# A recurrent attention feeding a gated MLP: one attention visit per chunk with two PSUM banks, one bank for the first MLP product, and x turned through memory

## The chip, the core and the metric

The kernel runs on one core of a Trainium2 chip. The core has TensorE (matrix products, results in PSUM, a memory of 8 banks of 512 fp32 values on each of 128 partitions), VectorE, ScalarE, GpSimd (which doesn't reach PSUM), and SyncE, whose queue (SP) issues most DMA transfers. The engines run their own instruction lists in order and wait for one another by semaphores. The metric is the device time of one execution in microseconds; lower is better.

## What is computed

There are 4 batches, 8 heads, 768 steps and a head width of 48. A recurrence over the steps gives y:

```python
state = np.zeros((B, H, D, D))
for t in range(S):
    cur = np.einsum('bhd,bhe->bhde', u[None] * k[:, :, t], v[:, :, t])
    y[:, :, t] = np.einsum('bhd,bhde->bhe', r[:, :, t], state + cur)
    state = w[None, :, :, None] * state + np.einsum('bhd,bhe->bhde', k[:, :, t], v[:, :, t])
```

With x = y laid out as 4 x 768 x 384, an MLP along the time axis of low rank (32) and one along the channels follow:

```python
h = xt @ U @ V                       # xt: x with time and channel exchanged
u = x + h.transpose(0, 2, 1)
out = u + np.maximum(u @ w_ch1, 0.0) @ w_ch2   # 384 -> 1536 -> 384
```

U, V, w_ch1 and w_ch2 arrive as 64-bit floats.

## The kernel before

**Attention.** Each batch is cut into 6 chunks of 128 steps, each of two sub-chunks of 64. Heads go in pairs: an even head lies on the lower 64 partitions, an odd head on the upper 64. For a chunk n, `p_sc` makes the scores of r and k and `p_su` the products of k and v that go into the state; both write the banks `pab` (PSUM tags `tr` and `sc`, one for each of two halves). VectorE reads them: `a_am` masks the scores, `a_st` makes the next state. `p_out` then makes the output rows: masked scores times v (`av`, with `vsw` a copy of v of the odd heads with sub-chunks exchanged), and r times the state (`sq`). All are matmuls of at most 64 x 64, which use only a quarter of the array each; the program alternates two lists of them (`in_turn`) that stand in different row halves of the array.

A chunk is done in two TensorE operations, the two parts of `a_part` (L864). Each alternates one row half of chunk n's output with the other half of chunk n+1's scores and state products. Both parts accumulate into one bank, `pav` (tag `av`, for every other chunk of batch 0 `mm`). Since two row halves may not write one bank at once, a copy of one element of `pav` by ScalarE or VectorE (`seen`, L903) stands between the parts: the second part's first matmul waits for it. `a_x` (L925) adds `pav` and the diagonal term `dv` into x.

**Between attention and MLP.** G = Uᵀx is summed over the batch's chunks: in batch 0 chunk by chunk in the bank of the wake matmuls (`c_gx`, `c_g0`), in the others in one operation (`c_g`, bank `pG`). u must stand with channels on partitions, split into a high part `uTh` in the type fp32r and the rest `uTl`. For the first half of a batch's steps, `c_x` (L1027) turns x with nine TensorE transposes into three banks, and `c_xu` (L1041) accumulates V·G on top and splits. For the second half of batches 1 to 3, `c_u` adds h to x, `c_store` writes it to memory in blocks of 32 x 32, `c_blocks` reads it back, and `c_turn` turns the blocks on VectorE.

**MLP.** All matmuls are fp32r with operands split in two. One unit is `m_1` (L1102): a first product of 9 matmuls of 128 x 128 x 384 into a bank of tag `mm` (two of them), then ScalarE's relu into `hh` and VectorE's `hl` = max(p, 0) - `hh`, which reads the bank again; and `m_2`: 9 matmuls into three `acc` banks. The units are issued as m_1(0), m_1(1), m_2(0), m_1(2), m_2(1) and so on, 24 pairs for each batch. Before each batch's first m_2 three matmuls V·G (`gate`) open the `acc` banks. In batch 0 each weight block is also loaded, turned from 64-bit floats (`raw_w`, on ScalarE and VectorE) and split into `w1s` and `w2s`.

**The order.** A planner in the program (class `Plan`) gets every operation with an engine, a cost estimate, its buffers and a due time, and lays out each engine's list by simulating the engines: an engine takes the ready operation with the earliest due time. An operation that may run on GpSimd or VectorE (`on_either`) goes where it would be done sooner. Due times are set in units of PER = 1.95: batch 0's MLP starts at T0 = 46, its attention chunks are 5.5 apart (EACH), those of batch 1 are 8 apart and those of batches 2 and 3 are 11. So a batch's attention is woven into the MLP of the batch before it. While batch 0 starts up, the planner puts dummy matmuls (`wake`, `wake2`) into gaps of TensorE.

The eight PSUM banks before: `mm` 2, `acc` 3, `tr` 1, `sc` 1, `av` 1.

Of the kernel before, what the change touches and what calls it, by code (L numbers as in the profile page):

```python
# [9 lines left out]
F32 = mybir.dt.float32  # L10
# [278 lines left out]
def rwkv_moe(ctx: ExitStack, tc: tile.TileContext, r, k, v, w, u, U, V, w1, w2, out):  # L289
# [42 lines left out]
    def bank(tag, name):  # L332
        return Buf(ps, [128, 512], F32, tag, {"mm": 2, "acc": 3}.get(tag, 1), name)
# [5 lines left out]
    opened = []  # L339

    def whole(*args, **kw):

        opened.clear()
        return nc.tensor.matmul(*args, **kw)  # L344
# [285 lines left out]
    def a_load(n):  # L630
        b, c = divmod(n, NCH)
        if n < 4:
            t3 = xbuf([128, 2 * H * HP + DM], F32, "uTl" if n % 2 else "uTh", 2, f"ld_{n}")

            def part(i):
                if i < 2:
                    return t3.t[:, i * H * HP:(i + 1) * H * HP].rearrange("p (h d) -> p h d", h=H)
                return t3.t[:, 2 * H * HP:].rearrange("p (h d) -> p h d", h=H)
            ts = [(t3, i) for i in range(3)]
# [13 lines left out]
        for i, src in enumerate((r, k, v)):  # L653
            eng = "ACT" if n < 3 and i == 1 else "SP"
            dma(lambda q, i=i, src=src: q.dma_start(part(i)[:, :, :D], src[b, :, c * C:(c + 1) * C, :].rearrange("h p d -> p h d")),  # L655
                [ts[i] if n < 4 else (t3, i)] if n < 4 else [(ts[i], "d")], [], 1024, 192, eng=eng)
        rs[n], ks_[n], vs[n] = [((lambda i=i: part(i)), ([(t3, i), (t3, f"pad{i}")] if n < 4 else [(ts[i], "d"), (ts[i], f"pad{i}")])) for i in range(3)]
# [69 lines left out]
    def a_tr(n, i):  # L727
# [18 lines left out]
        def turn(q0, q1):  # L746
            opened.clear()
# [34 lines left out]
    avp = {}  # L782
# [26 lines left out]
    ROWS = (1, 0)  # L809

    def p_out(n, row):
# [4 lines left out]
        pt = avp[n]  # L816
# [5 lines left out]
        def av(q, j, i):  # L822
# [3 lines left out]
                                    start=(row == ROWS[0] and q == 0), stop=False, skip_group_check=True)  # L826

        def sq(q, i):
            rows = head_rows(row)
            return nc.tensor.matmul(to(q, row, i), lhsT=rT.t[rows, q, i * C2:(i + 1) * C2], rhs=St[n, i].t[rows, q, :],  # L830
                                    start=False, stop=(row == ROWS[1] and q == NP - 1), skip_group_check=True)
# [15 lines left out]
    def reads(n, j, i):  # L847

        return [*trs[n], kss[n], *vs[n][1]]

    seen = {}

    def a_first(n):

        abs_[n] = [bank(t, f"pab_{n}_{j}") for j, t in enumerate(AB)]
        a, b_ = p_sc(n, 0) + p_su(n, 0), p_sc(n, 1) + p_su(n, 1)
        pe(1000, lambda: in_turn(a, b_), abs_[n], reads(n, 0, 0), tiled=True)
        ams[n] = [None, None]
        for j in range(2):
            a_am(n, j)  # L860
        for i in range(2):
            a_st(n, i)

    def a_part(n, part):  # L864

        nxt = (n + 1) % NCH
        last = n % NCH == NCH - 1
        row = ROWS[part]
        if part == 0:
            if nxt:  # L870
                abs_[n + 1] = [bank(t, f"pab_{n + 1}_{j}") for j, t in enumerate(AB)]
            avp[n] = bank("mm" if front(n) and n % 2 else "av", f"pav_{n}")
        o = 1 - row
        mine = p_out(n, row)
# [520 lines left out]
```

## Time and profile before

| what | value |
|---|---|
| median of 3 runs | 427.16 us (426.8 to 429.48) |
| span of the profiled execution, first to last instruction | 426.3 us |
| TensorE busy | 415.6 us, 98% |
| VectorE, ScalarE, GpSimd busy | 264.5, 137.3, 63.6 us |
| relu `hh`, 96 times on ScalarE | 47.1 us |
| `hl`, 96 times on VectorE | 53.0 us |
| first MLP matmul of batch 0 | 53.65 us |

The page gives the profiled execution by its span; its own time is not listed beside it. In the profile a busy TensorE means that some matmul was under way; since matmuls overlap, the distance between starts tells what one costs, not its length. `Lnnn` is a line of the kernel; MLP matmuls all stand at L344 (a helper), so tiles tell them apart: `p` is an MLP product, `pab` and `pav` belong to attention, `pu`, `ph` and `pG` to the step between. The small fp32 matmuls of attention leave two records each.

### The profile page before, as it was taken

The numbers are of one execution on the slowest core, as the hardware profiler recorded it, in microseconds if no ns is written. First come the engines' busy times: TensorE is split into PE (matmuls) and PEld (weight loads), VectorE is DVE, ScalarE is ACT, GpSimd is POOL, SyncE is SP. The second block draws the span as 40 slices with busy tenths as digits, with TensorE's granted clock in tenths as the row PEclk, the third lists the DMA queues.
The fourth block names the chain that finished last, engine by engine and source line by source line (L and its number), as shares of the span: only waits on it lengthen the run. The fifth ranks groups of instructions, "written<-read, shape, count | busy, mean of one in ns | idle before, by whom it ended". The sixth has DMA issues, their size and how long they took to land.

```text
span 426.3 us, 12170 instructions
## 1 busy us (share of the span) xinstructions
PE 415.6 (98%) x5122; PEld 397.3 (93%) x5122; DVE 264.5 (62%) x598; ACT 137.3 (32%) x374; POOL 63.6 (15%) x100
## 2 busy tenths in 40 slices
PE   8998999999999999999999999999999999999994
PEld 8888899999999999999999999999999999999994
DVE  6888897599999838676785466576622452113122
ACT  2876695276541314112112221322112221111110
POOL 2654220053521003011100001101100000000000
PEclk9998899999999999999999999999999999999999
DMA  9979977697458676755477664231100420001001
GB/s 144 157 148 246 250 177 147 158 260 179 83 85 180 113 162 102 139 90 84 104 147 118 104 153 60 47 66 31 57 2 2 75 92 2 0 0 58 0 2 62
DMA packets 181951, 43.53 MB, mean 102 GB/s; under 512 B 168961, under 2 KB 180354, under 8 KB 181890
## 3 DMA queue, kind: packets, MB, share of 16 engines
q1 hardware_dynamic: 176706, 41.21, 48.2%
q10 hardware_dynamic: 5184, 1.48, 1.9%
q8 instruction: 42, 0.69, 0.7%
q14 instruction: 19, 0.16, 0.1%
HBM read 36.18 MB, written 6.49 MB: 100 GB/s over the span
## 4 chain that ended last, share of the span: by engine, by line
PE 84%; DMA 5%; SPq 5%; DVE 2%; ACT 1%; issue 1%; DVEq 0%; ACTq 0%
PE p L344 72%; SPq L655 4%; PE pav L824 4%; DMA raw_w<-in_moe_w_ch_dram 3%; PE pav L830 3%; PE pab L788 2%; PE pu L344 1%; DMA ub<-in_u_dram 1%; PE pab L803 1%; SPq L515 1%; DMA wT<-in_w_dram 1%; PE pG L995 1%; SPq L667 1%; DMA raw_v<-in_moe_V_dram 1%; DVE raw_w L543 0%
## 5 line engine op out<-in xcount | busy, mean ns | idle before, releaser
L344 PE MATMUL p<-uTh,w1s 128*128 128x384 f32 x576 | 148.2, 338 | 0.0
L1118 DVE SCALAR_TENSOR_TENSOR hl<-p,hh 128x384 fp32r<-128x384 f32 x96 | 53.0, 552 | 113.7 <-ACT hh L1117 113.5
L344 PE MATMUL p<-w2s,hh 128*128 128x384 f32 x576 | 119.3, 340 | 0.0
L1117 ACT ACTIVATE hh<-p 128x384 fp32r<-128x384 f32 x96 | 47.1, 490 | 207.2 <-PE p L344 207.2
L344 PEld LDWEIGHTS p<-uTh,w1s 128*128 128x128 f32 x576 | 103.0, 188 | 0.8
L344 PEld LDWEIGHTS p<-w2s,hh 128*128 128x128 f32 x576 | 99.9, 188 | 1.6
L344 PE MATMUL p<-uTl,w1s 128*128 128x384 f32 x288 | 96.5, 335 | 0.0
L344 PE MATMUL p<-w2s,hl 128*128 128x384 f32 x288 | 65.9, 334 | 0.0
L344 PEld LDWEIGHTS p<-uTl,w1s 128*128 128x128 f32 x288 | 54.0, 188 | 0.3 <-DVE uTl L1050 0.3
L344 PEld LDWEIGHTS p<-w2s,hl 128*128 128x128 f32 x288 | 51.4, 188 | 0.0
L824 PE MATMUL pav<-vsw,am 64*64 64x48 f32 x384 | 32.9, 224 | 0.1
L824 PEld LDWEIGHTS pav<-vsw,am 64*64 64x64 f32 x384 | 26.5, 136 | 5.5 <-issue 3.5
L788 PE MATMUL pab<-rT,kT 48*64 48x64 f32 x768 | 31.0, 226 | 0.4 <-issue 0.2
L830 PE MATMUL pav<-S,rT 48*64 48x48 f32 x704 | 31.3, 220 | 0.0
L830 PEld LDWEIGHTS pav<-S,rT 48*64 48x64 f32 x704 | 27.3, 137 | 0.0
L824 PE MATMUL pav<-ldv,am 64*64 64x48 f32 x320 | 26.5, 222 | 0.8 <-ACT seen L903 0.8
L824 PEld LDWEIGHTS pav<-ldv,am 64*64 64x64 f32 x320 | 21.5, 134 | 5.7 <-issue 4.2
L788 PEld LDWEIGHTS pab<-rT,kT 48*64 48x64 f32 x768 | 24.9, 136 | 1.7 <-issue 1.3
L698 POOL MEMSET ks<- 128x128 f32 x24 | 4.9, 205 | 137.6 <-PE pav L830 50.4
L922 DVE TENSOR_TENSOR am<-pab,mask 128x256 f32<-128x256 f32 x48 | 19.6, 416 | 6.5 <-PE pav L830 5.8
L803 PE MATMUL pab<-ldv,ks 64*48 64x48 f32 (+1 forms) x576 | 21.4, 214 | 0.0
L803 PEld LDWEIGHTS pab<-ldv,ks 64*48 64x48 f32 (+1 forms) x576 | 19.0, 130 | 0.0
(133 smaller groups left out, 500.7 us busy)
## 6 DMA issues: line engine op xcount, KB each, us to landing
raw_w<-in_moe_w_ch_dram SPq DMA_DIRECT2D x24, 384.0 KB, 5.0
out_dram<-x SPq DMA_DIRECT2D x21, 192.0 KB, 2.1
ldr<-in_r_dram SPq DMA_DIRECT2D x20, 192.0 KB, 3.4
ldk<-in_k_dram SPq DMA_DIRECT2D x20, 192.0 KB, 3.8
ldv<-in_v_dram SPq DMA_DIRECT2D x20, 192.0 KB, 3.8
bl<-in_r_dram SPq DMA_DIRECT2D x79, 48.0 KB, 2.8
bl<-in_k_dram SPq DMA_DIRECT2D x79, 48.0 KB, 2.4
vsw<-in_v_dram SPq DMA_DIRECT2D x42, 48.0 KB, 3.0
```

The lines of the kernel that those rows point to most:

```text
L344: return nc.tensor.matmul(*args, **kw)
L515: mine.append(q.dma_start(view(raw.t[p0:p0 + ap.shape[0]]), ap.bitcast(I32) if wide else ap))
L655: dma(lambda q, i=i, src=src: q.dma_start(part(i)[:, :, :D], src[b, :, c * C:(c + 1) * C, :].rearrange("h p d -> p h d")), [ts[i] if n < 4 ...
L667: dma(lambda q, i=i, s0=s0: q.dma_start(t.t[(1 - i) * C2:(2 - i) * C2], v[b, 1::2, s0:s0 + C2, :].rearrange("h p d -> p h d")), [(t, i)], ...
L698: op("POOL", 250, lambda: nc.gpsimd.memset(ks.t[:, :, D:], 0.0), [(ks, "pad")], [])
L788: return [lambda q=q, i=i: nc.tensor.matmul(pt.t[(i ^ j) * C2:(i ^ j) * C2 + C2, q * C2:(q + 1) * C2], lhsT=kT.t[rows, q, i * C2:(i + 1) * ...
L803: return nc.tensor.matmul(pt.t[j * HP:j * HP + m, SU + q * D:SU + (q + 1) * D], lhsT=ks.t[half, 2 * q + j, :m], rhs=vt()[half, 2 * q + j, ...
L824: return nc.tensor.matmul(to(q, j, i), lhsT=am[j].t[half, q, :], rhs=vsw[n].t[half, q, :] if j else vt()[half, 2 * q, :], start=(row == RO ...
L830: return nc.tensor.matmul(to(q, row, i), lhsT=rT.t[rows, q, i * C2:(i + 1) * C2], rhs=St[n, i].t[rows, q, :], start=False, stop=(row == RO ...
L922: on_dve(256, lambda e: e.tensor_tensor(am.t, abs_[n][j].t[:, :SU].rearrange("p (h t) -> p h t", h=NP), mask_.unsqueeze(1).broadcast_to([1 ...
L1117: on_act(384, lambda: nc.scalar.activation(hh.t, pt.t[:, :TB], AF.Relu), [hh], [pt])
L1118: on_dve(384, lambda e: e.scalar_tensor_tensor(hl.t, pt.t[:, :TB], 0.0, f32(hh.t), ALU.max, ALU.subtract), [hl], [pt, hh])
```

## The change

- `a_part` becomes `a_visit`: one TensorE operation for each chunk. It first alternates both halves of chunk n+1's scores and state products, then both row halves of chunk n's output. Each row half accumulates into a bank of its own (`pav0`, `pav1`), which exist once for the whole run and are set to zero by VectorE at the start. `seen` goes, with its wait and the matmul that stood for it where no other did. `a_x` adds the two banks in two VectorE operations.
- The `mm` tag has one bank. The relu goes into a buffer `hr` in SBUF, ScalarE copies it into `hh`, and `hl` is `hr` - `hh` on VectorE or GpSimd.
- In batches 1 to 3 the x of the first half goes through memory too: `c_store` and `c_blocks` ahead of time, `c_turn_x` turns the blocks on VectorE, and `c_xu` adds V·G from PSUM to it and splits.
- Batch 0 keeps its TensorE transposes; those of its second half move into `c_xu`, and two banks (`sc`, `tr`) serve its three columns. `c_u` has two banks too.
- v of the first four chunks gets a tile of its own in the place of `hl` buffers.

The banks after: `mm` 1, `acc` 3, `tr` 1, `sc` 1, `pav` 2.

```diff
     def bank(tag, name):
-        return Buf(ps, [128, 512], F32, tag, {"mm": 2, "acc": 3}.get(tag, 1), name)
+        return Buf(ps, [128, 512], F32, tag, {"acc": 3}.get(tag, 1), name)
...
-    ROWS = (1, 0)
+    pav = [Buf(ps, [128, 512], F32, None, 1, f"pav{row}") for row in range(2)]
...
-        pt = avp[n]
+        pt = pav[row]
...
-                                    start=(row == ROWS[0] and q == 0), stop=False, skip_group_check=True)
+                                    start=(q == 0), stop=False, skip_group_check=True)
...
+    def begin_chunk(n):
+
+        abs_[n] = [bank(t, f"pab_{n}_{j}") for j, t in enumerate(AB)]
+        return [p_sc(n, j) + p_su(n, j) for j in range(2)]
+
+    def taken(n):
+
+        ams[n] = [None, None]
+        for o in range(2):
+            a_st(n, o)
+            a_am(n, o)
...
-    def a_part(n, part):
+    def a_visit(n):
 
         nxt = (n + 1) % NCH
...
+        wr = list(pav)
+        mine = [p_out(n, row) for row in range(2)]
+        other = [[], []]
         if nxt:
...
+            other = begin_chunk(n + 1)
+            rd += reads(n + 1)
+            wr += abs_[n + 1]
+
+        def visit():
+            in_turn(*other)
+            in_turn(*mine)
+        pe(1750 if nxt else 900, visit, wr, rd, tiled=True)
         if nxt:
-            a_st(n + 1, o)
-            a_am(n + 1, o)
-        if part:
-            a_x(n)
+            taken(n + 1)
+        a_x(n)
...
-        on_dve(384, lambda e: e.tensor_tensor(x.t, pt.t[:, :DM], dv.t.rearrange("p h d -> p (h d)"), ALU.add),
-               [x], [pt, dv])
+        for row, more in ((0, lambda: dv.t.rearrange("p h d -> p (h d)")), (1, lambda: x.t)):
+            on_dve(384, lambda e, row=row, more=more: e.tensor_tensor(x.t, pav[row].t[:, :DM], more(), ALU.add),
+                   [x], [pav[row], dv])
...
+    def c_turn_x(b, ct):
+
+        bt = ublk.pop((b, 0, ct))
+        xt = xTs[b, ct] = wbuf([128, TB], F32, "xl", NXS, f"xT_{b}_{ct}")
+        on_dve(384, lambda e: e.transpose(xt.t.rearrange("p (j t m) -> p j m t", t=32, m=4),
+                                          bt.t.rearrange("p j (m c) -> p j m c", c=32)), [xt], [bt])
...
         for ct in range(NCT):
-            pt = upt[b, t][ct]
+            if b == 0 and t:
+                for i in range(TPB):
+                    c_x(b, t, ct, i)
+            pt = upt[b, t, ct] if b == 0 else bank(("sc", "tr")[ct % 2], f"pu{b}_{t}_{ct}")
...
+            if b:
+                xt = xTs.pop((b, ct))
+                on_dve(384, lambda e, xt=xt, pt=pt: e.tensor_tensor(xt.t, pt.t[:, :TB], xt.t, ALU.add), [xt], [pt])
+                on_act(384, lambda ct=ct, xt=xt: nc.scalar.copy(uh.t[:, ct, :], xt.t), [(uh, ct)], [xt])
+                on_either(384, lambda e, ct=ct, xt=xt: e.tensor_tensor(ul.t[:, ct, :], xt.t, f32(uh.t[:, ct, :]),
+                                                                       ALU.subtract), [(ul, ct)], [xt, (uh, ct)])
+                continue
...
-        on_act(384, lambda: nc.scalar.activation(hh.t, pt.t[:, :TB], AF.Relu), [hh], [pt])
-        on_dve(384, lambda e: e.scalar_tensor_tensor(hl.t, pt.t[:, :TB], 0.0, f32(hh.t), ALU.max, ALU.subtract),
-               [hl], [pt, hh])
+        hr = xbuf([128, TB], F32, "hr", 2, f"hr_{b}_{t}_{f}")
+        on_act(384, lambda: nc.scalar.activation(hr.t, pt.t[:, :TB], AF.Relu), [hr], [pt])
+        on_act(384, lambda: nc.scalar.copy(hh.t, hr.t), [hh], [hr])
+        on_either(384, lambda e: e.tensor_tensor(hl.t, hr.t, f32(hh.t), ALU.subtract), [hl], [hr, hh])
...
+    for p in pav:
+        at(-101, lambda p=p: on_dve(512, lambda e: e.memset(p.t, 0.0), [p], []))
...
-            at(t, lambda n=n: a_part(n, 0))
-            at(t + per / 2, lambda n=n: a_part(n, 1))
+            at(t, lambda n=n: a_visit(n))
...
+            for i in range(TPB):
+                at(t0 + per * (i + 1) + 0.1, lambda b=b, i=i: c_store(b, i))
+            for ct in range(NCT):
+                at(t0 + per * TPB + 2 + ct, lambda b=b, ct=ct: c_blocks(b, 0, ct))
+                at(t0 + per * TPB + 8 + ct, lambda b=b, ct=ct: c_turn_x(b, ct))
...
-            for i in range(TPB):
-                at(t + 2 + 0.1 * i, lambda i=i: c_x(0, 1, i))
             at(t + 3, lambda: c_xu(0, 1))
         else:
-            for i in range(3):
-                at(end + 0.1 + 0.1 * i, lambda b=b, i=i: c_x(b, 0, i))
             at(end + 1, lambda b=b: c_xu(b, 0))
```

More of the change, by code (lines that the diff above doesn't have):

```diff
@@ L830, in sq @@
             return nc.tensor.matmul(to(q, row, i), lhsT=rT.t[rows, q, i * C2:(i + 1) * C2], rhs=St[n, i].t[rows, q, :],
-                                    start=False, stop=(row == ROWS[1] and q == NP - 1), skip_group_check=True)
+                                    start=False, stop=(q == NP - 1), skip_group_check=True)
         for q in range(NP):
@@ L845, in in_turn, with reads @@
                     l[k_]()
-    def reads(n, j, i):
+    def reads(n):
         return [*trs[n], kss[n], *vs[n][1]]
-    seen = {}
-    def a_first(n):
[L855 to L862, printed above, removed]
@@ L864, in a_part @@
-    def a_part(n, part):
-        nxt = (n + 1) % NCH
[L867 to L874, printed above, removed]
-        other = p_sc(n + 1, o) + p_su(n + 1, o) if nxt else []
-        def first():
-            in_turn(mine, other)
-            opened.append(n)
-        def second():
-            if opened:
-                whole(avp[n].t[:, DM:DM + 1], lhsT=ident_, rhs=ident_[:, :1], start=False, stop=False, skip_group_check=True)
-            i = mine[0]()
-            tc.add_manual_dep(i.ins, seen.pop(n).ins.name,
-                              mybir.DependencyInfo(mybir.DependencyClass.Sync, mybir.DependencyReason.DATA),
-                              reason="one bank for both halves of the rows")
-            in_turn(other[:1], [])
-            in_turn(mine[1:], other[1:])
+    def begin_chunk(n):
+        abs_[n] = [bank(t, f"pab_{n}_{j}") for j, t in enumerate(AB)]
+        return [p_sc(n, j) + p_su(n, j) for j in range(2)]
@@ L894, in a_part @@
         if nxt:
-            rd += reads(n + 1, o, o)
-            wr += [abs_[n + 1][o]]
-        t = None
-        if part == 0:
-            pe(600 if last else 1000, first, wr, rd, tiled=True)
-            t = wbuf([128, 1], F32, "seen", 2, f"seen_{n}")
-            def see(copy):
-                seen[n] = copy(t.t[C2:C2 + 1], avp[n].t[C2:C2 + 1, (7 + row) * D - 1:(7 + row) * D])
-            one_of([("ACT", 150, lambda: see(nc.scalar.copy), False), ("DVE", 130, lambda: see(nc.vector.tensor_copy), False)],
-                   [t], [avp[n]])
-            seens[n] = t
-            if nxt:
-                ams[n + 1] = [None, None]
-        else:
-            pe(600 if last else 1000, second, wr, rd + [seens[n]], tiled=True)
@@ L1318, in rwkv_moe @@
     for i in range(3):
-        at(end - 2 + 0.1 * i, lambda i=i: c_x(0, 0, i))
+        at(end - 2 + 0.1 * i, lambda i=i: [c_x(0, 0, ct, i) for ct in range(NCT)])
     for b in range(B):
```

37 lines of the change are left out of this document (17 added, 20 removed).

## The prediction

> **What bounds the kernel now.** I read the busy table first, then busy time by stage, then the chain of waits, and last the timeline of single stretches. Columns of the stage table: stretch in us, its length, busy us of TensorE (PE), its weight loads (PEld), VectorE (DVE), ScalarE (ACT) and GpSimd (POOL) with instruction counts, granted clock, DMA share, GB/s.
>
> ```profile
> span 426.3 us, 12170 instructions
> PE 84%; DMA 5%; SPq 5%; DVE 2%; ACT 1%; issue 1%; DVEq 0%; ACTq 0%
> ...
> 40.40:53.80 13.40, 12.37 (x166) 11.30 (x157) 12.04 (x22) 7.96 (x19) 5.14 (x7) 0.87 1.03 264
> 53.80:92.00 38.20, 38.20 (x369) 36.93 (x368) 30.29 (x64) 23.86 (x61) 7.17 (x9) 1.00 0.82 179
> 92.00:142.00 50.00, 49.80 (x797) 46.38 (x795) 49.36 (x113) 22.66 (x62) 16.27 (x21) 1.00 0.71 143
> 326.00:420.60 94.60, 94.52 (x589) 94.02 (x588) 27.28 (x52) 18.54 (x39) 1.01 (x1) 1.00 0.10 26
> ...
> 332.92 87.62 PE p L344 x505
> ```
>
> From 53.8 to 420.6 us TensorE has work in all but 0.3 us of the stretches shown, at full clock, and it holds 84% of the chain. In the last row 505 MLP matmuls follow one another in 87.6 us, so one costs 0.1735 us. In this long part a microsecond of TensorE work saved is a microsecond of time, as long as nothing new makes TensorE wait. Before 53.8 us it is otherwise: there loads, the recurrence of batch 0 and the splitting of weights decide, the clock falls to 0.87, and TensorE fills gaps with dummy matmuls. One stretch has a second engine at its limit: from 92 to 142 us VectorE is busy 49.36 of 50 us.
>
> **1. Two parts become one visit.** In the chain, each row is a start, a length and the work:
>
> ```profile
> 203.14 4.89 PE p L344 x27
> 209.10 4.89 PE p L344 x27
> 215.06 4.89 PE p L344 x27
> ...
> 160.40 0.62 PE pab L788 x32
> 219.95 0.60 PE pav L824 x16
> ```
>
> From one of these rows to the next lie 5.96 us, with 27 MLP matmuls (27 x 0.1735 = 4.68) and one attention part in it; a part costs 1.28 us. The first gap holds a part that mixes its own products with those of the next chunk, the second a part of a batch's last chunk, which has only its own: the same price for half the records. The last two rows say why: 32 records that alternate between both row halves of the array take 0.62 us, 16 on one half take 0.60. What lies inside a mixed part:
>
> ```profile
> 201.99 0.25 PE L824 MATMUL pav<-ldv,am 64*64 64x48 f32 x1
> ...
> 202.92 0.22 PE L803 MATMUL pab<-ldv,ks 64*64 64x48 f32 x1
> 203.07 1.31 PE L344 MATMUL p<-w2s,hh 128*128 128x384 f32 x6
> ```
>
> The small matmuls start over 201.99 to 202.94, 0.95 us; the other 0.33 of the 1.28 is paid on going in and out. The Trainium skill, TensorEngine Tiling (Array Packing), Key Properties, says that changing the tiling mode drains TensorE, and gives no time for it; by that rule the border is paid per change of mode, and the 0.33 agrees.
>
> After the change, chunks 0 to 4 of batches 1 to 3 have one border instead of two: 15 x 0.33 = 5.0 us less. The last chunk of each has both row halves at work together, one part's 1.28 us in place of two: 3 x 1.28 = 3.8 us less. The records themselves stay. I take 8.8 us. Bounds: 3.8 if the border is paid again between the two lists of the visit; for pairs of halves that don't overlap, see the rivals. The new visit waits for four VectorE operations of the visit before and for both adds into x, with the MLP queued behind it on TensorE; parts are now 5.96 us apart and visits will be about twice that, the four operations some 1.5 us, so it costs nothing there. The tiny copy "seen" and its wait go; its cost lies in batch 0 (item 4).
>
> **2. The turns of x leave TensorE.** For batches 1 to 3 nine transposes each go:
>
> ```profile
> 233.02 1.14 PE L344 MATMUL pu<-ident,x 128*128 128x128 f32 x9
> 233.92 0.77 PE L344 MATMUL pu<-V,Gs 96*128 96x384 f32 x3
> ...
> L1091 DVE STREAM_TRANSPOSE ut<-ub 128x384 f32<-128x384 f32 x9 | 7.2, 858 | 0.0
> ud<-x SPq DMA_DIRECT2D x9, 192.0 KB, 3.4
> ub<-ud SPq DMA_DIRECT2D x9, 192.0 KB, 3.7
> ...
> 193.47 0.55 DVE L929 TENSOR_TENSOR x<-pav,dv 128x384 f32<-128x384 f32 x1
> ```
>
> From 233.02 to 233.92: 0.90 us, 2.7 us for three batches, all on the path. In their place come nine stores and nine loads (3.4 and 3.7 us to land, each also an issue on SP's queue, where the next batch's loads stand behind) and nine VectorE transposes of 0.86 us, 7.7 us in all. In batch 2 the third chunk's x is there at 194.0 (last row) and is wanted at 233.9; 3.4 + 3.7 + 3 x 0.86 = 9.7 us fits four times. A store that waits on SP for a late x delays loads which are issued a chunk or more ahead. Cost zero while that holds. The V·G matmuls stay; behind them an add replaces a subtraction on VectorE and the subtraction goes to either engine. Only batch 0's second half now turns its third column inside the stretch, since two banks serve three columns: three transposes and a matmul, 3 x 0.10 + 0.17, about +0.4.
>
> **3. One bank for the first product.** The next first product may begin only when ScalarE's relu has emptied the bank. Rows of the last stretch and of the start of batch 0's MLP:
>
> ```profile
> 414.31 0.49 ACT L1117 ACTIVATE hh<-p 128x384 fp32r<-128x384 f32 x1 [2.63 <-PE p L344]
> 415.68 0.51 PE L344 MATMUL p<-uTh,w1s 128*128 128x384 f32 x2
> ...
> 55.48 0.51 PE L344 MATMUL p<-uTh,w1s 128*128 128x384 f32 x2
> 55.68 0.49 ACT L1117 ACTIVATE hh<-p 128x384 fp32r<-128x384 f32 x1
> 57.04 0.69 PE L344 MATMUL p<-Gs,V 96*128 96x384 f32 x3
> ```
>
> In the steady order a second product of 9 matmuls lies between: the bank is free at 414.31 + 0.49 = 414.80 and wanted at 415.68, 0.88 us to spare. At a batch's start two first products stand back to back: the second starts at 55.48, and would have to wait for 55.68 + 0.49 = 56.17, about 0.7 us with the handover. Four batches: 2.8 us at most. The three gate matmuls (last row, 3 x 0.17 us) need no relu and can move into the gap, which leaves 4 x 0.2 = 0.8. I take 1.5, between the two. Bounds: 0.8 and 2.8, more if relus come late (rivals).
>
> The hidden vector becomes: relu into SBUF, a second ScalarE copy, then a subtraction on GpSimd or VectorE. ScalarE gets 96 more copies of 0.49, some 47 us; from 326 on it is busy 18.54 of 94.6 us, so there is room. The subtraction is ready one copy later than now, with a first and a second product (3 us) between its relu and its use. If that cover went, each of 96 units could lose up to a copy. The second add into x puts 24 x 0.55 us on VectorE and two clears of a bank run while it waits for its first load. VectorE in all gets some 21 us more, or less where GpSimd takes subtractions; 142 on has room, 92 to 142 has not (rivals).
>
> **4. The start of batch 0.** Rows of its last chunk, of the matrix G, and of the first MLP matmul:
>
> ```profile
> 42.67 0.25 PE L824 MATMUL pav<-vsw,am 64*64 64x48 f32 x1
> 45.46 0.25 PE L824 MATMUL pav<-ldv,am 64*64 64x48 f32 x1 [0.83 <-ACT seen L903]
> 46.64 0.56 DVE L929 TENSOR_TENSOR x<-pav,dv 128x384 f32<-128x384 f32 x1
> 51.44 0.55 DVE L985 TENSOR_TENSOR Gs<-wake,Gs 32x384 fp32r<-32x384 f32 x1
> 53.54 3.00 DVE L1050 TENSOR_TENSOR uTl<-pu,uTh 128x384 fp32r<-128x384 f32 x6
> 53.65 0.51 PE L344 MATMUL p<-uTh,w1s 128*128 128x384 f32 x2
> ...
> 65.65 1.04 POOL L581 TENSOR_TENSOR w1s<-raw_w,w1s 128x384 fp32r<-128x384 f32 x1 [8.36 <-ACT w1s L580]
> 70.47 0.46 ACT L1117 ACTIVATE hh<-p 128x384 fp32r<-128x384 f32 x1
> ```
>
> The last chunk's second part starts 2.8 us after the first, held by "seen", which sat behind weight work on ScalarE. One visit from 42.67 ends near 43.9, two adds near 45.0 instead of 47.2: x is 2.2 us earlier, and G can be. Against it: the one bank passes from the wake matmuls to the first product only when the third low part of u is there, 53.54 + 3 x 0.5 = 55.0 in place of 53.65, +1.35. Earlier chunks may gain too. But the weights limit it: the sixth w1 is split at 66.7, and its product, whose relu starts at 70.47, begins at about 70.47 - 0.37 - 8 x 0.1735 = 68.7 (0.37 from the last matmul to the relu: 414.31 less 413.94, where that matmul starts 10 x 0.1735 before 415.68). So no more than 2.0 can be used unless splits come sooner too. I take 1.5 less; bounds 1.35 more and 4 less (both waits of the recurrence gone and splits 2 us sooner).
>
> **Sum.** -8.8 - 2.7 + 0.4 + 1.5 - 1.5 = -11.1. The profiled execution spans 426.3 us; the runs' median is 427.16, 0.9 above it, which I take for what lies around the span. 426.3 + 0.9 - 11.1 = 416.1.
>
> **Rivals.** *A, helpers hold it back.* VectorE has 0.64 us free in 92 to 142 and gets there five or six adds, three transposes of 0.86 and an added second input from SBUF in the subtraction. If GpSimd takes that, these rows count:
>
> ```profile
> 47.56 1.21 POOL L699 TENSOR_TENSOR ks<-ldk,tab 128x384 f32<-128x384 f32 x1 [4.45 <-DMA ldk<-in_k_dram]
> 47.82 1.38 DVE L543 SCALAR_TENSOR_TENSOR raw_w<-raw_w 128x384 int32<-128x384 int32 x1
> 50.86 0.55 DVE L543 SCALAR_TENSOR_TENSOR raw_w<-raw_w 128x384 int32<-128x384 int32 x1
> ```
>
> The same VectorE operation takes 1.38 beside a GpSimd one and 0.55 without, +0.83. Six subtractions before the sixth w1 then cost 6 x 0.83 = 5.0 against the 2.0 to spare: weights 3 late. And batch 1's attention may end late and eat its gain (3.7). 416.1 + 3 + 2, about 421. For it: both margins. Against: some of VectorE's work in 92 to 142 is for batch 2 and can slip. The rule of the Trainium skill that speaks here is in GPSIMD Engine Reference, Specifications: GpSimd shares its SBUF interfaces with VectorE, with contention for instructions with two SBUF inputs. By that rule the new subtraction, unlike the old one that reads PSUM, is itself slowed; the three rows agree for the older operations.
>
> *B, the bank waits recur.* If the relu starts 1.2 us late in the steady order instead of 0.37, 0.88 becomes 0.05; at 1.4 late each of some 45 units without a visit between loses 0.15, +7: 423. Against: ScalarE had waited 2.63 us idle for TensorE in the row above.
>
> *C, slower.* Two row halves that both write outputs, in any pairing that the trace does not show, may not overlap. The 32 records of each half then take 0.60 x 4 = 2.4 in place of 1.24 for the output half of 18 visits: +1.2 x 15 and +1.2 x 3, some 21 us: 416.1 + 21 = 437. It decides from 0.6 us a visit on. Against: the row at 160.40 overlaps halves in two banks, and outputs go to two banks now.
>
> That TensorE does not get less to do cannot be: visits are one operation each and the turns are gone.
>
> **Chances.** Forecast 0.68 (its own range 411 to 420), A 0.17, B 0.07, C 0.05, and 0.03 for a schedule that comes out no better, about 427. What a measurement of this kernel tells from no change is about 1%, 4.3 us. Faster by more: 0.68 + 0.17 x 0.75 + 0.07 x 0.4 = 0.84; within 1%: 0.10; slower: 0.06. The range 411 to 422 leaves out C, the last case, half of B and the ends of the others, 2 in 10.
>
> **What would show it.** Right: 53.8 to the end with TensorE as full as now; visits at about 2.2 us, the last chunk's at 1.3; no turns of x after batch 0; gaps before first products only at batch starts, under 0.7 us; the first MLP matmul near 52. Wrong: idle TensorE ahead of first products with ScalarE as releaser (B), a stall for w1s or a late G with VectorE full (A), visits of 3 us and more (C).

## The result, and the profile after

The median after the change is 422.9 us (422.63 to 424.94, 7 runs) against 426.85 (426.43 to 429.48, 7 runs) for the kernel before: ratio 0.9913, 95% interval 0.9888 to 0.9939. The change gains 4.0 us where 11.1 were forecast, and the time lies 0.9 above the range. The profiled execution took 422.63 us with a span of 420.9.

The stage table of the kernel after, in the columns of the prediction's table (stretch, length, busy us of TensorE, its weight loads, VectorE, ScalarE, GpSimd, granted clock, DMA share, GB/s); the last stretch ends at its own last matmul:

```profile
40.40:53.80 13.40, 8.14 (x183) 7.50 (x178) 12.96 (x23) 9.03 (x23) 8.38 (x9) 0.92 1.04 266
53.80:92.00 38.20, 36.77 (x259) 35.24 (x260) 30.66 (x65) 27.60 (x68) 2.89 (x4) 0.94 0.84 193
92.00:142.00 50.00, 49.63 (x891) 47.65 (x891) 49.01 (x111) 30.37 (x85) 20.88 (x23) 1.00 0.72 145
326.00:415.30 89.30, 89.18 (x512) 88.43 (x511) 26.66 (x51) 30.52 (x62) 0.00 (x0) 1.00 0.11 28
```

From 92 us on TensorE is as full as before. The loss is visible in the first two rows: TensorE has 8.14 us of work in 13.4 (12.37 before), and in the second row it idles 1.4 us and the clock is 0.94. The chain of waits shows the visits (start, length, work):

```profile
188.83 9.57 PE p L341 x54
198.40 0.62 PE pab L784 x32
199.03 0.40 PE pab L799 x25
199.48 0.45 PE pav L822 x29
199.95 0.47 PE pav L828 x30
200.41 8.01 PE p L341 x45
...
210.41 9.57 PE p L341 x54
219.98 0.61 PE pav L822 x32
220.59 0.47 PE pav L828 x32
221.06 8.01 PE p L341 x45
```

With the prediction's 0.1735 us for an MLP matmul, the first visit costs 200.41 - 188.83 - 54 x 0.1735 = 2.21 us, where the forecast needs 2 x 1.28 - 0.33 = 2.23; the last chunk's costs 221.06 - 210.41 - 9.37 = 1.28, as forecast. To set the two ends of the run apart I use one event that both kernels have: the start of the third first product of batch 0 (MLP matmuls in steady order from there), and the last matmul. Rows of TensorE's timeline (start, length, operation); before:

```profile
59.16 0.51 PE L344 MATMUL p<-uTh,w1s 128*128 128x384 f32 x2
420.18 0.34 PE L344 MATMUL p<-w2s,hl 128*128 128x384 f32 x1
```

and after:

```profile
65.23 0.62 PE L341 MATMUL p<-uTh,w1s 128*128 128x384 f32 x2
414.89 0.34 PE L341 MATMUL p<-w2s,hl 128*128 128x384 f32 x1
```

From the third product to the end: 361.02 us before, 349.66 after, 11.36 less. Up to it: 6.07 more. So the forecast gain is there to its size, and over half of it is lost before 65 us. The chain of the kernel after names the way there:

```profile
47.28 0.54 DVE dg L712
47.83 0.98 DVE raw_w L543
48.81 2.56 DVE raw_w L540 x2
...
53.61 0.56 DVE Gs L952
54.22 0.79 PE wake L341
...
55.37 1.24 ACT uTh L1034 x3
56.61 0.43 ACT w2s L577
57.04 0.76 ACT uTh L1034 x2
57.80 0.45 ACT raw_w L537
58.25 0.45 ACT raw_w L559
58.70 0.45 ACT raw_w L537
59.16 0.46 ACT raw_w L559
59.62 0.43 ACT w1s L577
60.04 0.48 ACT raw_w L537
60.52 0.42 ACT raw_w L559
60.95 0.47 ACT raw_w L537
61.41 0.39 ACT hr L1103
```

Two stretches of weight work lie in it. On VectorE x is complete at 47.37 (its second add starts at 46.82 and takes 0.55), and TensorE ends its last product for G at 48.32 (start 47.42, length 0.90; before, 49.30 and 1.21, so 50.51). Yet G's half follows only at 53.61, behind six `raw_w` operations that take up to 1.3 us each; before, four stood there. On ScalarE eight weight operations stand between the copies of u and the first relu, and the second first product (61.84) waits for that relu, since there is one bank. TensorE's own timeline there:

```profile
54.22 0.79 PE L341 MATMUL wake<-V 96*128 96x512 f32 x1 [5.68 <-DVE Gs L952]
57.91 0.74 PE L341 MATMUL p<-uTh,w1s 128*128 128x384 f32 x2
...
61.84 0.62 PE L341 MATMUL p<-uTh,w1s 128*128 128x384 f32 x2 [1.01 <-ACT hr L1103]
```

The bracket gives the idle time ahead and what ended it. The dummies `wake2` can't fill the 5.68 us now: their bank is the one that holds the sum G until G is read (the run with the wake bank, below, shows them in the gap with a bank of their own).

### The profile page after: what moved, and what is told of

Its sections match the earlier page's. It is cut to its first block, busy times and chain, and to the rows that moved or that the text cites. A ratio compares the mean times of both kernels' runs of the same rounds, so it can differ in the third digit from the quotient of the medians.

```text
span 420.9 us, 12333 instructions
## 1 busy us (share of the span) xinstructions
PE 402.0 (96%) x5111; PEld 388.6 (92%) x5111; DVE 280.6 (67%) x620; ACT 188.1 (45%) x482; POOL 75.6 (18%) x111
## 4 chain that ended last, share of the span: by engine, by line
PE 84%; DVE 5%; DMA 4%; ACT 3%; issue 1%; SPq 1%; ACTq 1%; DVEq 0%
PE p L341 70%; PE pab L784 3%; PE pav L822 3%; DMA vsw<-in_v_dram 3%; PE pav L828 2%; PE pab L799 2%; PE wake L341 1%; DMA raw_w<-in_moe_w_ch_dram 1%; SPq L653 1%; PE pG L962 1%; DVE raw_w L540 1%; ACT raw_w L537 1%; DVE uTl L1031 1%; ACTq L665 1%; PE ptk L746 1%
## 5 line engine op out<-in xcount | busy, mean ns | idle before, releaser
L1105 DVE TENSOR_TENSOR hl<-hr,hh 128x384 fp32r<-128x384 f32 x92 | 53.2, 579 | 111.2 <-ACT hh L1104 104.9
L1103 ACT ACTIVATE hr<-p 128x384 f32<-128x384 f32 x96 | 47.1, 491 | 179.0 <-PE p L341 176.7
L1104 ACT CAST hh<-hr 128x384 fp32r<-128x384 f32 x96 | 49.2, 513 | 2.6
L716 ACT ACTIVATE dv<-ldv,dg 128x48 f32<-128x48 f32 x104 | 25.2, 325 | 3.9 <-DVE dg L712 3.6
L784 PEld LDWEIGHTS pab<-rT,kT 48*64 48x64 f32 x768 | 13.4, 134 | 7.9 <-issue 4.2
L784 PE MATMUL pab<-rT,kT 48*64 48x64 f32 x768 | 16.7, 224 | 2.4 <-ACT tab L461 1.2
L341 PE MATMUL wake<-ident 128*128 128x128 f32 x116 | 17.2, 307 | 1.7 <-POOL ident masks.py:199 1.7
L341 PEld LDWEIGHTS wake<-ident 128*128 128x128 f32 x116 | 16.2, 221 | 1.7 <-POOL ident masks.py:199 1.7
L822 PE MATMUL pav<-vsw,am 64*64 64x48 f32 x384 | 17.2, 220 | 0.5 <-issue 0.5
L930 ACT ACTIVATE SW<-S,wm 112x48 f32<-112x48 f32 x56 | 14.2, 323 | 6.7 <-DVE S L917 5.0
L917 DVE TENSOR_TENSOR S<-pab,SW 112x192 f32<-112x192 f32 x40 | 14.0, 351 | 3.8 <-PE pab L799 3.4
```

Of the source, the lines that this page charges most:

```text
L716: nc.scalar.activation(dv.t[:, h], vt()[:, h], AF.Copy, scale=dg.t[:, h:h + 1])
L784: return [lambda q=q, i=i: nc.tensor.matmul(pt.t[(i ^ j) * C2:(i ^ j) * C2 + C2, q * C2:(q + 1) * C2], lhsT=kT.t[rows, q, i * C2:(i + 1) * ...
L822: return nc.tensor.matmul(to(q, j, i), lhsT=am[j].t[half, q, :], rhs=vsw[n].t[half, q, :] if j else vt()[half, 2 * q, :], start=(q == 0), ...
L917: on_dve(192, lambda e, new=new, ptv=ptv, dec=decayed[n, j]: e.tensor_tensor(new.t, ptv(), dec.t, ALU.add), [new], [pt, decayed[n, j]])
L930: nc.scalar.activation(dec.t[:, q], new.t[:, q], AF.Copy, scale=wm.t[:, q])
L1103: on_act(384, lambda: nc.scalar.activation(hr.t, pt.t[:, :TB], AF.Relu), [hr], [pt])
```

## The experiments

Each was timed in five rounds beside runs of the kernel before, except where one run is given. "The rest" is the time from the third first product to the start of the last matmul, from the profiled run; G is the start of its VectorE half. Each profile is one execution, and the start of batch 0 differs between executions: in the profile with 20 dummies (426.49 us, 3.5 above that kernel's median) and in the one with the second bank (425.18, 3.3 above) TensorE waits 3.42 and 2.06 us for a load of v ahead of V's spread, which then takes 2.84 and 2.85 us in place of 1.60. There the way from G to the third product tells more than G.

| kernel | G | third product | the rest | ratio to before, 95% |
|---|---|---|---|---|
| before (profile shown) | 51.44 | 59.16 | 361.0 | 1 |
| after | 53.61 | 65.23 | 349.7 | 0.9913 (0.9888 to 0.9939) |
| before, one bank | 51.27 | 61.20 | 361.0 | 1.0075 (1.0049 to 1.0102) |
| before, two banks, new evacuation | 48.99 | 56.71 | 361.4 | 1.0006 (0.9982 to 1.003) |
| after, G first | 52.20 | 65.01 | 349.2 | 0.9918 (0.989 to 0.9945) |
| after, GpSimd later | 51.38 | 63.92 | 349.8 | 0.9922 (0.9891 to 0.9953) |
| after, wake bank | 53.06 | 63.24 | 354.9 | 0.9982 (0.9954 to 1.001) |
| after, second bank | 55.28 | 64.55 | 350.8 | 0.9885 (0.9858 to 0.9912) |
| after, all four edits | 51.78 | 61.16 | 352.0 | 0.9834 (0.9805 to 0.9862) |
| all four, without signs | 51.56 | 61.77 | 349.3 | 0.9793 (0.9765 to 0.982) |
| after, 20 dummies | 56.98 | 68.77 | 350.0 | 0.9904 (0.987 to 0.9938) |
| after, relu first, 20 dummies | 53.92 | 64.28 | 352.5 | 0.9927 (0.9899 to 0.9955) |
| after, x on TensorE | 53.89 | 65.50 | 352.2 | 1.0009 (0.998 to 1.0038) |

### The kernel before once more

No edit; one run.

> The kernel before, unchanged, profiled once more, to tell what lies around a span and how typical the first profile is. Theory: a run's time is its span + 1.7 us; at a time near the median, 426.8, the span is 425.1 and the second first product starts near 54.3 in place of 55.48. Rival: the first profile is typical (second first product at 55.5, work after it 365.0 us), and the 1.2 us lie elsewhere.

It took 430.03 us with a span of 428.3, so 1.7 lies around a span, as for the kernel after (422.63 and 420.9). The prediction put 0.9: the execution shown of before (426.3) took about 428.0, some 1.2 above its median. This run is on the slow side as well and gives no typical start. It shows something else: TensorE idled 1.81 us waiting for G, the clock then was 0.5 from 53 to 56.4, and G to the third product took 9.05 us instead of 7.72.

```profile
51.81 1.32 PE L344 MATMUL pu<-V,Gs 96*128 96x384 f32 x6 [1.81 <-DVE Gs L985]
```

### The one bank alone, and the new evacuation alone

In the kernel before: `"mm": 2` taken out, relu into `hr`, copy into `hh`, `hl` from both (the lines of the change's diff), odd chunks' `pav` in tag `av`, v of the first chunks in its own tile; and the same with two banks, where the odd chunks' `pav` stays in `mm`.

> The kernel before with the change's third part alone: one bank for the first product, the relu into SBUF, a second copy for hh, hl from SBUF on either engine; v of the first four chunks in its own tile, as hr needs the room. My prediction's term: +1.5 us (0.8 to 2.8), so 427.6 to 429.6 against 426.8. If the miss lies in this part (the bank held by the wake matmuls, the late second product): +3 to +5, 430 to 432, with the distance of the first two first products near 3.9 in place of 1.83 and the first one near 2 us later after G.

> The kernel before with relu into SBUF, second copy and hl from SBUF, but with its two banks for the first product (and the odd chunks of batch 0 in a bank of that tag, as before). It splits the +3.2 us that the one bank with the same evacuation cost. Theory bank: the bank carries it, so 426.6 to 427.6 here against 427. Rival copies (96 more copies of 0.5 us on ScalarE and the later hl carry it, through ScalarE's and GpSimd's share in splitting the weights): 429.5 to 430.5.

One bank: 430.6 us against 427.14, +3.2. Two banks with the same evacuation: 427.82 against 427.14, no difference clear of noise. So 96 more copies cost nothing that is clear of noise, and the bank, with the move of the odd chunks' `pav` that it brings, costs some 2.9. The rows of VectorE and TensorE with one bank show where:

```profile
51.27 0.55 DVE L986 TENSOR_TENSOR Gs<-wake,Gs 32x384 fp32r<-32x384 f32 x1
55.66 0.51 PE L344 MATMUL p<-uTh,w1s 128*128 128x384 f32 x2
57.97 0.62 PE L344 MATMUL p<-uTh,w1s 128*128 128x384 f32 x2
61.20 0.51 PE L344 MATMUL p<-uTh,w1s 128*128 128x384 f32 x2
422.18 0.34 PE L344 MATMUL p<-w2s,hl 128*128 128x384 f32 x1
```

From G to the third product 9.93 us instead of 7.72, +2.2; the rest is 361.0 as before. So the bank is paid at the start of batch 0, nearly nothing later; 0.7 of the 2.9 isn't placed. The prediction had 1.5 for it and 1.35 for the handing over from the wake matmuls, 2.85 together: right in size.

### Four edits of the start, one by one

G's VectorE half ahead of three weight blocks; GpSimd's `ks` and `dv` of the second chunk of batch 1 behind G; `wake2` in bank `sc`; the second first product in bank `tr`:

```diff
-                op("DVE", dve(n), sign, [(raw, "lo")], [(raw, "hi")], lock=True)
-                op("DVE", dve(n), join, [(raw, "lo")], [(raw, "hi")], lock=True)
+                later = [Gs[0]] if name in ("w1_2", "w2_1", "w1_3") else []
+                op("DVE", dve(n), sign, [(raw, "lo")], [(raw, "hi")] + later, lock=True)
+                op("DVE", dve(n), join, [(raw, "lo")], [(raw, "hi")] + later, lock=True)
...
-e.tensor_mul(ks.t[:, :, :D], kt()[:, :, :D], by_head(tab.t)), [(ks, "d")], kb + [tab],
+e.tensor_mul(ks.t[:, :, :D], kt()[:, :, :D], by_head(tab.t)), [(ks, "d")], kb + [tab] + ([Gs[0]] if n == 7 else []),
-e.tensor_mul(dv.t, rt()[:, :, :D], kt()[:, :, :D]), [dv], rb + kb,
+e.tensor_mul(dv.t, rt()[:, :, :D], kt()[:, :, :D]), [dv], rb + kb + ([Gs[0]] if n == 7 else []),
...
-    wk2 = bank("mm", "wake2")
+    wk2 = bank("sc", "wake2")
...
-        pt = bank("mm", f"p1_{b}_{t}_{f}")
+        pt = bank("tr" if (b, t, f) == (0, 0, 1) else "mm", f"p1_{b}_{t}_{f}")
```

> The changed kernel, with the VectorE operations that turn the weights w1_2, w2_1 and w1_3 into 32-bit form listed behind G's. My theory: batch 0's MLP starts late because G's VectorE half (53.61 us in the changed kernel, 51.44 before) stands in VectorE's queue behind them; ScalarE's half is done at 50.1. Then G's VectorE half starts near 50.2, the first MLP matmul near 54.5 instead of 57.9, and the time falls by about 3.4 us to 419.5. Rival: the supply of weights sets the start of the MLP anyway; then what is gained at G is lost in waits for w1s or w2s further on, and the time stays at 422.9 within 0.7.

> The changed kernel, with chunk 7's GpSimd work (ks and dv, 48.4 to 52.2 us) held until G is done. If GpSimd's use of SBUF stretches VectorE's weight operations (1.3 us each there, 0.55 elsewhere), the seven operations ahead of G's VectorE half take 0.47 each, that half starts near 51.1 instead of 53.6, and the time falls by 2.5 us to 420.4. If the stretch has another cause (the weights' transfers), they stay at 1.3 and the time at 422.9.

> The changed kernel, with the second set of dummy matmuls in the bank tagged sc, so that the one bank of the first product is free from G on. My theory: holding it until the third low part of u, and the idle 5.7 us before, in which the dummy matmuls cannot run and the clock falls, cost 2 us between G and the first MLP matmul (4.3 us, 2.2 before). Then that stretch takes about 2.3 us, no idle stretch over 2 us stands ahead of it, and the time falls by 2 us to 420.9. Rival: the low parts of u set the first matmul whatever the bank: 422.9.

> The changed kernel, with the second first product of batch 0 alone in the bank tagged tr. My theory: with one bank it waits for a relu that stands behind four weight operations on ScalarE (61.27 us, 1.7 after the last matmul), which costs 1.0 to 2.1 us. Then the second product follows the first within 2 us instead of 3.9 and the time falls by about 1 us to 421.9, less if the second MLP product then waits for hh instead. Rival: the wait just moves to hh and hl, and the time stays at 422.9.

Medians 422.76, 422.45, 425.85 and 421.88 against 426.55; the kernel after has 422.9. The first two gain 0.1 and 0.5 us where 3.4 and 2.5 were expected, and the third loses 2.9 where a gain of 2 was expected. The fourth comes where it was expected (421.9), though its interval still meets that of the kernel after, and its second product follows the first by 2.88 us in the profile, not within 2: pairs of matmuls take 0.84 us there, at the slow clock, in place of 0.51. With G first, the planner put products of batch 1 (`ks`, `dv`) on VectorE in the place of the weight operations, so G came at 52.20 and not near 50.2. With GpSimd later, VectorE's rows ahead of G are

```profile
48.92 1.01 DVE L540 SCALAR_TENSOR_TENSOR raw_w<-raw_w 128x384 int32<-128x384 int32 x2
51.38 0.55 DVE L952 TENSOR_TENSOR Gs<-wake,Gs 32x384 fp32r<-32x384 f32 x1
```

1.01 us for two operations that took 2.64 in the kernel after, beside GpSimd's products there:

```profile
49.63 1.32 POOL L704 TENSOR_TENSOR dv<-ldr,ldk 128x384 f32<-128x384 f32 x1
48.74 2.64 DVE L540 SCALAR_TENSOR_TENSOR raw_w<-raw_w 128x384 int32<-128x384 int32 x2
```

That is what makes G late: it comes 2.2 us sooner without it. But the third product comes only 1.3 sooner (63.92). From G to it 12.54 us pass in place of 11.62: the granted clock is 0.50 from 52 to 58 us, over most of the first product, and the second still waits 0.65 us for the relu on ScalarE.

With the wake bank the dummies run into the gap ahead of G for 2.75 us (from 47.90), and 3.01 us of idle time are left:

```profile
53.66 0.97 PE L341 MATMUL pu<-V,Gs 96*128 96x384 f32 x4 [3.01 <-DVE Gs L952]
```

The first product comes 2.55 us behind G as expected (4.30 in the kernel after). But the rest is over 5 us longer; TensorE's longest waits from 60 to 150 us (engine, what waited, for what, us in total, times, longest) are one without a named releaser and one for a weight:

```profile
PE p L341 <- issue: 1.9, 1, 1.9
PE p L341 <- ACT w1s L577: 1.4, 1, 1.4
```

### All four together, and two tries on top

> All four edits of the start together: G ahead of three weight blocks on VectorE, GpSimd's two last products behind G, the second wake matmuls in another bank, the second first product in another bank. Theory start (the 6.4 us lost at the start of batch 0 are TensorE time, each held by the others as long as one is left): second first product 4 to 6 us earlier than 61.84, time 417.5 to 419.5. Rival weights (the weight blocks come no faster, so an earlier start is lost again before 110 us): second first product as early, but TensorE idle 3 us and more for w1s or w2s between 85 and 110, time 421.5 to 423.

> As the kernel with all four edits, and batch 1's loads of r, k and v from its third chunk on due 6 us later, so that on SP's queue they stand behind the weights of the second half instead of ahead. Rival weights, by the queue: the idle time for w1s and w2s between 85 and 110 goes down by 2 us or more against the kernel with all four, time 419 to 420.5. Weights by the conversions on ScalarE and VectorE, not by the queue: no change, within 0.5 us of the kernel with all four. Theory start: no change either, since there is no such idle time.

> The kernel with all four edits of the start, with batch 1's attention due 4 us later (one constant, 34 to 38), so that VectorE's work for the weights of the second half meets less of the attention's. Theory VectorE: idle time before 110 us goes down by 1 to 2 us, time 418.8 to 420. Rival (VectorE is full up to 142 us whatever stands in which order, and batch 1 then starts late): 420.5 to 422, with TensorE waiting for G or u between 140 and 150.

All four: 420.58 us (419.39 to 421.06) against 427.14. This beats both kernels, and lies between the ranges of the two theories. The third product comes at 61.16, 4.07 us sooner than in the kernel after, and the rest is 2.3 longer: about half is given back. TensorE idles in it 1.43 us at 94.79, without a named releaser, and 0.76 at 124.08, for `w1s`. Neither later loads (422.61) nor a later attention of batch 1 (423.3) mends that; both lie above every range put for them, and why isn't shown. Their edits:

```diff
-                at(t0 + per * c - per - 16, lambda n=n0 + c: a_load(n))
+                at(t0 + per * c - per - (10 if b == 1 and c > 1 else 16), lambda n=n0 + c: a_load(n))
...
-            t0, per = ((begin[b - 1] + 34, 8.0), (begin[b - 1] + 8, 11.0))[b > 1]
+            t0, per = ((begin[b - 1] + 38, 8.0), (begin[b - 1] + 8, 11.0))[b > 1]
```

### Less VectorE work on the weights

All four edits, and the operation that puts signs into the second half's weight blocks left out:

```diff
+                half2 = name[:2] in ("w1", "w2") and int(name[3:]) >= 6
+                if not half2:
-                op("DVE", dve(n), sign, [(raw, "lo")], [(raw, "hi")] + later, lock=True)
+                    op("DVE", dve(n), sign, [(raw, "lo")], [(raw, "hi")] + later, lock=True)
```

> The kernel with all four edits of the start, without the VectorE operation that puts the sign into the 12 weight blocks of the second half of the channels (12 x 0.55 = 6.6 us of VectorE work between 75 and 115 us less; those weights come out positive). Theory VectorE (the weights' supply is held by a full VectorE, and through it the earlier start is given back): TensorE's idle time from 84 to 142 us goes from 2.2 to under 0.7 us, time 1.5 to 3 us below the kernel with all four, 417.6 to 419.1. Rival (the loads or ScalarE hold the weights): idle time and time within 0.7 us of the kernel with all four.

418.47 us, 2.1 below the kernel with all four. The stage table from 84 to 142 us, with all four and then without signs:

```profile
84.00:142.00 58.00, 55.80 (x981) 53.13 (x981) 54.88 (x125) 36.03 (x98) 19.02 (x24) 1.00 0.82 176
```

```profile
84.00:142.00 58.00, 58.00 (x1028) 55.45 (x1030) 54.42 (x120) 39.75 (x108) 20.52 (x25) 1.00 0.82 176
```

TensorE's idle 2.2 us are gone, and the rest is 349.3, as short as in the kernel after with its later start. So what gives an earlier start back is VectorE's share in the supply of weights; ScalarE has 20 us free in the stretch.

### The clock

Behind the last turn of x before G, dummies into columns of that bank that nobody reads, 45 and then 20:

```diff
+            if (b, t, ct, i) == (0, 1, 1, 2):
+                for _ in range(20):
+                    whole(upt[b, t, ct].t[:, DM:], lhsT=ident_, rhs=ident_, start=False, stop=False,
+                          skip_group_check=True)
```

> The changed kernel with one edit: 45 dummy matmuls of 128 columns behind the last turn of x that TensorE makes before it waits for G, into columns of that bank that nobody reads (some 4.7 us by the spacing of such rows); the order of all other instructions is the same. Theory clock (the idle 5.68 us before G drop the granted clock to 0.5 for about two stretches of 3.4 us, and the MLP starts in them): no clock below 0.9 after 54 us, the first nine matmuls of the MLP 0.17 apart from the start, second first product 1.5 to 2.5 us earlier than 61.84, time 420.5 to 421.5. Rival (the clock costs nothing, since the weights and relus set the pace of the first units): clock as high, time 422.4 to 423.4.

> As the kernel with 45 dummies, with 20: there each took 0.227 us (10.21 us by its row, two records each), so that they ran on 4.7 us beyond G; 20 take 4.5 us and end before G. Theory clock: no clock below 0.9 after 54 us if the dummies end under 2 us before G; from the first V x G matmul to the third first product 2 us less than now (54.22 to 65.23 in the changed kernel), the rest of the run 350.0 us as there; time 420.5 to 421.5 against 422.9. Rival (the clock costs nothing): time 422.4 to 423.4.

> The 20 dummies, and GpSimd's two last products of the second chunk of batch 1 behind G. Theory (three separate losses at the start, each TensorE time until VectorE's supply of weights binds): G's VectorE half ends 2.8 us after x in place of 6.8, clock full at the MLP's start, third first product at 61 to 62.5 in place of 65.23, the rest 350 to 352; time 418.5 to 420.5. Rival (the supply binds at once): time not below 421.5, the rest 352.5 and more.

45 dummies took 10.21 us, twice what I had put, and ran on beyond G: third product 70.65, time 427.6. A start 5.4 us later costs 4.7; the rest stays at 349.7. With 20 the clock stays up. The stretch from the first matmul behind G to the end of the first product, in the kernel after and with 20 dummies (columns as in the stage table):

```profile
54.22:59.72 5.50, 5.50 (x19) 4.95 (x20) 4.76 (x10) 4.36 (x11) 0.00 (x0) 0.62 0.95 226
```

```profile
58.26:62.86 4.60, 4.34 (x22) 3.37 (x21) 3.63 (x8) 3.90 (x10) 0.00 (x0) 1.00 0.82 188
```

The stretch is 0.9 us shorter, and yet the time is 422.96: the theory of the clock alone falls. From G to the third product it is 11.79 us (11.62 without dummies), for TensorE now waits longer for the relu:

```profile
65.38 0.62 PE L341 MATMUL p<-uTh,w1s 128*128 128x384 f32 x2 [1.41 <-ACT hr L1108]
```

With GpSimd later as well (423.24 us) that wait is 2.16, the clock falls again behind it (0.53 from 62 to 64 us), and the third product comes at 65.39, 14.61 us behind G, where 61 to 62.5 was expected.

### ScalarE's list

The first weight operations of four blocks wait for the first relu (`hr0` keeps it); then the same with 20 dummies, and with GpSimd later too:

```diff
+            first = [hr0[0]] if name in ("w1_4", "w2_3", "w1_5", "w2_4") else []
...
-                op("DVE", 100 + 0.65 * n, on_dve_byte, [(raw, "lo")], loaded, lock=True,
+                op("DVE", 100 + 0.65 * n, on_dve_byte, [(raw, "lo")], loaded + first, lock=True,
...
-                                                       scale=2.0 ** -112), [(raw, "hi")], loaded)
+                                                       scale=2.0 ** -112), [(raw, "hi")], loaded + first)
```

> The changed kernel with one edit: the first weight operations of four blocks (the second halves' turn from 64-bit floats that stood between the copies of u and the first relu on ScalarE) wait for the first product's relu, so that ScalarE takes that relu first. Theory ScalarE's list (the second product waits for the one bank, that for the relu, that for eight weight operations ahead of it, whatever TensorE's clock does): with the clock still at 0.5 until 58.4 the first product ends near 59.7, relu at 60.1 in place of 61.27, second first product 60.6 in place of 61.84; time 421.5 to 422.4. Rival (the weights then come later by as much): 422.6 to 423.5.

> The same, with the 20 dummies that keep the clock up. Alone those changed nothing (422.96). Theory (clock and ScalarE's list stand side by side over the same 7.6 us from G to the second product, so that only both together free it): from the first dummy behind G to the second first product 5 to 6 us in place of 7.6 (7.1 with dummies alone), time 420 to 421.5. Rival (something else holds it): within 0.6 us of the kernel with the relu first alone.

> The same, with GpSimd's two last products of the second chunk of batch 1 behind G as well, so that G comes 2 us sooner. Theory: all three waits of the start shortened with one bank; third first product at 60 to 62 in place of 65.23, the rest 350 to 352.5; time 418.5 to 420.5, as far as with the second bank (420.6). Rival (the weights bind, so the sooner G is given back): no lower than the kernel without this edit.

423.91, 423.82 and 423.88 us against 427.64: no gain; the first lies above both ranges put for it, the others where their rivals had them. With the dummies the way from G to the third product is 10.36 us in place of 11.62, so the list and the clock together do hold a part of it; but the rest is 352.5 instead of 349.7. TensorE's waits in it are for the relu, 1.3 us in all, 1.06 of them at the start of batch 1 (150.34); none is for a weight, so that putting the weights off costs the 2.8 isn't shown. In the third kernel even the first relu is held by the weights, through a weight copy ahead of it (ScalarE, then TensorE):

```profile
59.69 0.53 ACT L578 CAST w2s<-raw_w 128x384 fp32r<-128x384 f32 x1 [2.61 <-DVE raw_w L543]
60.66 0.62 PE L341 MATMUL p<-uTh,w1s 128*128 128x384 f32 x2 [1.59 <-ACT hr L1110]
```

### The turns of x alone

The kernel after with `c_x` back in `c_xu` for all batches and `c_store`, `c_blocks`, `c_turn_x` of the first half taken out:

```diff
-            if b == 0 and t:
+            if b or t:
                 for i in range(TPB):
                     c_x(b, t, ct, i)
-            pt = upt[b, t, ct] if b == 0 else bank(("sc", "tr")[ct % 2], f"pu{b}_{t}_{ct}")
+            pt = upt[b, t, ct]
```

> The changed kernel with the second part undone alone: in batches 1 to 3 x of the first half is turned by nine TensorE transposes each, in two banks for three columns, and no longer through memory. My prediction's term: 2.7 us more, 425.2 to 426 against 422.9, and VectorE some 10 us less busy. Rival (the way through memory costs VectorE or SP so much that undoing it gains something back): 423 to 424.5. Other way (three columns through two banks make TensorE wait): over 426.5, with waits of TensorE ahead of turns.

426.87 us, ratio 1.0009: 4.1 above the kernel after by the two ratios. In the profile the rest grows by 2.5 (65.50 to 417.66), near the 2.7 put for it. Of the other 1.6, 0.3 is a later third product, 0.7 lies behind the last matmul and 0.6 isn't placed. The time is above the 425.2 to 426 expected and in the range of the other way (over 426.5), but the sign of that isn't there: from 66 us on TensorE waits 0.4 us in all, and not ahead of a turn.

## Why the prediction was wrong

**Visits and turns of x** were right: 2.21 and 1.28 us a visit as worked out, 2.5 for the turns by undoing them, and 11.36 us in the profile from the third product on, against 8.8 + 2.7 put. One reading of item 1 is off by a gap: from 209.10 to 215.06 stands a part mixed with the scores of the last chunk, and the last chunk's own part follows, from 215.06 to the next row of MLP matmuls at 221.01. That is 5.95 us, so the price of 1.28 stands.

**One bank** was right in size (2.85 put with the handing over, some 2.9 measured) and wrong in place: its 1.5 was spread over four batch starts, and the run with one bank alone shows it nearly all in batch 0.

**The step that failed is item 4, the start of batch 0**: 1.5 us less was taken, from x 2.2 sooner and G with it, less 1.35 for the handing over, and the rest from a hope in earlier chunks for which it shows no row. The profile has the first MLP matmul at 57.91, where near 52 was put, and the third product 6.07 later than before. Of this:

- G comes 2.17 later. x was not sooner (47.37 in place of 47.20), as the last visit starts at 44.60 and not at 42.67. Ahead of it on TensorE stand V's spread, sums and turns of x without a gap from 41.54, and VectorE's second add for the chunk before reads one of its banks until 44.15; which of the two held it isn't told apart. TensorE's part of G was done 2.2 sooner all the same (48.32), and VectorE's list lost that and 2.17 more: two more weight operations stand ahead of G, and they stretch to 1.3 us beside GpSimd's products; with these moved, G comes at 51.38. The row of 1.38 against 0.55 was in the prediction, but used for rival A's subtractions only.
- The bank adds 2.2, as it does alone.
- The remaining 1.7 lies between the first and the second product (3.93 us, 2.31 with the one bank alone). It is in the main the relu behind eight weight operations and the halved clock, side by side: taking either away alone shortens the way by at most 0.8 (11.79 and 10.82, from G at 54.28 to 65.10, against 11.62), both together by 1.26. The last 0.4 stays open.

**The cover that was missed**: the prediction named the dummies as TensorE's filler, but not that their bank is now held until G is read. TensorE idles 5.68 us; the price of the slow clock itself turned out to be hidden behind the relu (lifting it gains nothing alone, and 0.5 once the relu comes first).

**Rival A** came in part: its sign, a late G with VectorE full, is there (12.96 of 13.40 us busy, G at 53.61), but by the weight operations, not by the adds and subtractions that it priced. It is also what binds next, and sooner than put. The prediction took a start up to 2.0 us earlier than before as usable, judged by the sixth w1; with all four edits the third product still comes 2.0 later than before (61.16 against 59.16), and 2.3 are lost already, at 94.79 and 124.08, until VectorE has less to do. Rivals B and C did not come: TensorE waits for `hr` once, 1.0 us in all, and row halves overlap.

**The base** was off too: 1.7 us lie around a span and not 0.9, so the profiled execution of before stood 1.2 above its median, and the steps worked out on it gain less against the median (5.4 in the profiles, 4.0 in the medians).

## What to carry to other kernels

When a change takes a bank or buffer away, look for everything that used it as cover, dummies included, and ask what may now run only after the last reader. Where several lists run side by side at a start, one wait taken away may show little (here +2.9 to -1.0 us one by one, -2.3 all together); undo them together once before calling a cause dead. And an earlier start is worth only what the supply behind it can follow: measure the steady part from a fixed event, so that gain and give-back can be told apart.

## What the runs showed of the hardware

- The slow clock comes in pieces. By stretches of 2 us a dip to 0.50 lasted 3.4 us after an idle of 1.8 us (53.0 to 56.4 in the second profile of before) and 6.8 after the 5.68 us of the kernel after (51.6 to 58.4). The Trainium skill, TensorE: Matmul & The Clock Gate, Part 1, tells of a free-running window of about 3.4 us and half rate after an idle window; the lengths agree, but here less than a whole idle window was enough. Not each such idle did it: behind 1.4 us (20 dummies, at 65.38) and 1.9 us (wake bank, at 96.93) the clock stayed at 1.00.
- Alone on the path such a dip cost 1.3 us (9.05 against 7.72); beside a longer wait it cost nothing (the kernel after, where the dummies that lift it gain nothing).
- A VectorE operation on `raw_w` of 128 x 384 goes from 0.5 to 1.3 us beside a GpSimd product, and the product from 1.0 to 1.3 (VectorE: rows of the kernel with GpSimd later and of the kernel after; GpSimd: 1.01 at 42.22 and 1.32 at 49.63 in the kernel after).
